# A hand-written plan of 1623 steps, in another order behind the 329th, with the loads of values issued by SyncE

## The chip, the core and the metric

The kernel runs on one core of one Trainium2 chip. The core has a matrix engine (TensorE; PE in the profile, its weight loads PEld), a vector engine (VectorE, DVE), an activation engine (ScalarE, ACT), a general engine (GpSimd, POOL) and SyncE (SP), which here issues transfers and nothing else. Each runs its own instructions in order, and they wait for one another by semaphores. Transfers between the main memory and the on-chip memory (SBUF) are carried out by 16 DMA engines; SP, ACT and POOL issue them here. TensorE writes into PSUM, a small memory whose banks the kernel names 0 to 3, beside two double ones.

The metric is the device time of one execution in microseconds, the median of several runs.

## What is computed

Four batches of eight heads, 768 positions of 64 numbers each. Every query and key is assigned to the nearest (by angle) of 16 centroids of its head, and a query attends only to the keys of its own cluster. What comes out goes, all heads side by side (512 numbers per position), through a two-layer network with SiLU between.

```python
# in _attn_ref: q_n, k_n and c_n are q, k and centroids divided by their lengths
B, H, S, D = q.shape
scale = 1.0 / np.sqrt(D)
...
q_assign = np.argmax(np.einsum('bhsd,hcd->bhsc', q_n, c_n), axis=-1)
k_assign = np.argmax(np.einsum('bhsd,hcd->bhsc', k_n, c_n), axis=-1)
mask = q_assign[:, :, :, None] == k_assign[:, :, None, :]
scores = scale * np.matmul(q, k.transpose(0, 1, 3, 2))
scores = np.where(mask, scores, -1000000000.0)
scores = scores - np.max(scores, axis=-1, keepdims=True)
attn = np.exp(scores)
attn = attn / (np.sum(attn, axis=-1, keepdims=True) + 1e-09)
return np.matmul(attn, v).astype(np.float32)
...
# in _moe_ref: x is that with the heads side by side, 3072 x 512
h = x @ w_in
g = h * (1.0 / (1.0 + np.exp(-h)))
return (g @ w_out).astype(np.float32)
```

## The kernel before

**The plan.** The kernel is scheduled by hand. After a short opening, a text of 1623 words (`plan`) is read from the first to the last, and each word is handed to `step`, which emits the instructions of one small piece of work. A word is a name, a number, and behind the point an engine letter (A for ACT, D for DVE, P for POOL) or the numbers of the PSUM banks that the step opens. Each engine gets its instructions in the order of the words, and what a step waits for follows from the tiles that it reads and overwrites. So the order of the words sets the order within each engine and each queue; between engines only the data decide, and an engine may run far ahead of another one's place in the text.

**A head, from load to output.** A job is one head of one batch (`h8` to `h31` behind the first eight, which have names of their own). Its words, in the order in which they depend on each other:

- `r` (L92) loads its queries and keys, two transfers on SP, into one of four `raw` buffers.
- `hi` (L103 on ACT, L105 on POOL, L107 on DVE) casts them to half precision; `lo` (L112, DVE) makes the rest that the cast lost.
- `ht` (L121) transposes both by a DMA transpose on SP, into `ab`. The first jobs use TensorE for that.
- `l` and `L` (L159, TensorE: 12 and 24 small matmuls) multiply with the centroids; `ls`, `mx` and `ge` (L168, L188, L197, all DVE) sum, take the maximum and mark the winner.
- From head 16 on the marks go on by `cs` (L204 and L205, POOL), `cx` (L213, a DMA transpose on SP into `cdt`) and `cv` (L217, a transfer that POOL issues) into `ab`, next to the transposed queries and keys. Before head 16 they go by `cm` (L226, TensorE), `ce` (L237 or L239) and a transfer on SP (L240).
- `qk` (L336) makes scores for 256 keys by 384 queries, two matmuls, with the marks as extra rows, so that pairs of different clusters come out hugely negative; `ex` (L341, ACT) takes the exponential into one of 13 `P` buffers. There are 192 of each. The scores go to one of two double banks.
- `vl` (L271) loads the values of a head into one of five `vn` buffers, issued by POOL where the word has the letter P, and by SP otherwise. `v` casts them (L277 on ACT, L279 on DVE or POOL) and frees that buffer.
- `pv` (L353, 36 matmuls) multiplies two heads' weights with their values; `nm` (L363 and L365, DVE) divides by the sums into one of three `xn` buffers.
- `xd` (L392) transposes that by a DMA transpose on SP into `xt`; `pt` and `pe` (L374 on TensorE, L383 or L385) do the same for some of them.

A batch has two halves of queries (`c` = 0 and 1), and four `xd` or `pe` fill `xt` of a half. The words `pv`, `nm` and `xd` count 8 for a batch: 8 to 11 are the first half of the second batch, 12 to 15 its second half, 24 and 25 the first two of the fourth.

**The network.** For the first two batches `e` (L401, four matmuls) multiplies a half's `xt` with one of 16 blocks of `w_in`, `t` (L413, ACT) takes the tanh and `g` (L416, DVE) makes the SiLU from it. The words `e48` to `e63` are the second half of the second batch. For the last two batches the first layer is done with seven products instead of eight: `ws` and `T` make sums of weights and inputs, `y` (L467, two matmuls) is one product, `u` (L479 to L483) combines them, `s` (L489, ACT) takes the SiLU. The second layer is `b` for the first rows and then `m` (L559, eight matmuls), seven products each for eleven pairs of row blocks, with `S` (L572) for the sums, `z` (L581) and `o` (L587 or L590) to bring results out and to store them (`bo`, L504, and L594, L596).

**What the letters do.** For `hi`, `v`, `ce`, `pe`, `u` and `vl` the engine letter chooses the engine. For `z` and `o` the function takes no letter:

```python
elif op == "vl":
    load_v(n, nc.gpsimd if eng == "P" else nc.sync)
elif op == "z":
    duos[n // 10].snap(n % 10)
elif op == "o":
    duos[n // 10].out(n % 10 // 2, n % 2)
```

Of the kernel before, what the change touches and what calls it, by code (L numbers as in the profile page):

```python
# [29 lines left out]
def kernel(  # L30
# [655 lines left out]
    def step(op, n, eng, banks):  # L686
# [167 lines left out]
        e53.1 t53 g53 pv16.0 nm16 qk104 ex128 ht24 g59 m22.3 qk103 ex104 ex103 S21 qk124 ht25 ex124 m21.1 z20.A hi27.D
        qk112 cs23 l24.0 e55.2 S22 ls24 mx24 S24 r28 o20 qk102 ex112 ge24 t55 g55 ex102 hi26.A lo26 m26 cv20 qk109
        ex109 z21.A qk110 pv17.0 cs22 ex110 qk108 cx22 ex108 lo27 m25 z22.A nm17 qk126 ex126 e51.3 vl23.P cv22 qk111
        vl22 t51 g51 r30 v20.P e50.2 l25.0 ex111 t50 g50 qk127 ex127 qk113 v21.D e49.3 v22.D ex113 t49 hi28.P lo28 m23
        qk116 ex116 pv18.2 g49 nm18 cs24 qk115 qk130 ls25 v23.A ex115 e52.3 t52 g52 ht26 cx23 vl30.P mx25 m31.2 ex130
        o21.A e57.0 t57 qk114 ex114 l26.3 g57 cx24 ge25 ls26 e62.1 t62 g62 cv23 qk117 ex117 e54.0 t54 g54 qk119 ex119
        e61.3 e48.1 t61 g61 vl25.P xd16 mx26 ge26 qk118 xd18 ex118 t48 g48 m27.0 o23 vl27.P vl29.P qk138 pv19.3 ex138  # L860
        ht27 cv24 qk121 ex121 cs25 m24 qk125 ex125 qk123 ex123 hi30.D S33 nm19 m37 qk122 ex122 l27.1 ws9 ws10 r29 cx25
        ht28 lo30 S43 qk120 ex120 z30.A m41.3 z40.D qk129 ex129 ls27 ht30 S31 S41 S32 xd17 pv20.1 nm20 xd19 qk142
        ex142 qk133 ex133 m36 z31.A cs26 qk132 ex132 ws0 ws1 o22 pv21.1 mx27 ge27 cs27 qk135 l28.0 ls28 S34 S42 nm21
        ex135 hi29.D qk136 m35 ex136 v27.D qk140 ex140 r31 cx27 lo29 qk134 ex134 m32.0 o30 qk137 ws2 m47 ws11 ex137
        cx26 z32.D qk143 ex143 qk139 ex139 pv22.1 qk141 o33 m33 ws4 ex141 xd21 pv23.0 ht29 mx28 nm22 S44 qk146 ex146
        ge28 cv25 qk149 ex149 nm23 xd22 l30.1 m46 z41.D v29.D cv27 qk145 ls30 xd23 ws3 hi31.D ex145 mx30 qk144 xd20
        lo31 y161.0 m45 qk155 ex144 z42.A o43 ex155 cv26 l29.1 ls29 mx29 qk147 ex147 m34 qk154 ex154 ge29 ws12 qk150
        ex150 m44 T20 qk148 ex148 o31.D ws13 ge30 T21 y167.1 u160.A u161.A y177.4 u170.D m43 ht31 cs28 T22 y171 ws5
# [59 lines left out]
```

## Time and profile before

| what | us |
|---|---|
| three runs | 297.0, 297.87, 299.0 |
| their median | 297.87 |
| the profiled execution, whole | 297.27 |
| its span, first to last instruction | 295.5 |
| PE busy, DVE, ACT, POOL | 285.6, 225.7, 241.4, 69.9 |

The profile shows one execution. The time of a run is a little longer than the span (297.27 against 295.5). "Busy" is the time in which at least one instruction of an engine ran. Matmuls overlap one another, so that the mean duration of one (326 ns for one of 384 columns) is about twice the distance at which they follow each other: in the chain of work that ended last, four such matmuls take 0.65 us. That distance is the cost of a matmul here, and the text calls it its pace. "Idle before, releaser" is the time in which an engine stood still ahead of an instruction, and what ended it. For a transfer the profile has two times: how long the queue of the issuing engine was taken by the issue, and when the data had landed, counted from the issue.

### The profile page before, as it was taken

Reading aid. Unit: us, or ns where it says so; the run is one execution under the profiler, and the core shown is the slowest. Engines: PE = TensorE matmul, PEld = TensorE weight load, DVE = VectorE, ACT = ScalarE, POOL = GpSimd, SP = SyncE. Lnnn points to the kernel's source line nnn. Section 1 sums busy time; section 2 is a strip of 40 time slices with the busy share of each in tenths; the row PEclk is TensorE's granted clock in tenths of the full one; section 3 lists DMA queues with packets and bytes.
Section 4 is the critical chain, followed back from the end, with each engine's and each line's share of the span. In section 5 each row is a group of like instructions: output and inputs, shape, how many; then the busy total and the mean of one; then the engine's idle time right before and its main releaser. Section 6 shows DMA issues by size and latency. Waiting matters only on the chain.

```text
span 295.5 us, 8542 instructions
## 1 busy us (share of the span) xinstructions
PE 285.6 (97%) x3401; PEld 209.1 (71%) x3401; DVE 225.7 (76%) x498; ACT 241.4 (82%) x422; POOL 69.9 (24%) x126
## 2 busy tenths in 40 slices
PE   8899999999999999996999999999999999999995
PEld 3767766676677887664777788766678777656884
DVE  5898949689999898887877889897756243788571
ACT  5999999965989888996998888789899999487531
POOL 2655814310200126560463202111300000000000
PEclk9999999999999999999999999999999999999999
DMA  6999999998798999795865695844100202300032
GB/s 208 289 268 248 194 205 177 231 270 184 143 311 163 215 181 183 216 234 134 182 175 173 158 144 135 102 125 133 49 10 28 78 10 75 123 3 0 14 113 89
DMA packets 75208, 44.12 MB, mean 149 GB/s; under 512 B 54289, under 2 KB 70961, under 8 KB 75169
## 3 DMA queue, kind: packets, MB, share of 16 engines
q1 hardware_dynamic: 70272, 35.75, 50.2%
q0 software_dynamic: 4608, 7.54, 13.7%
q8 instruction: 26, 0.43, 0.7%
q10 hardware_dynamic: 288, 0.30, 0.3%
q14 instruction: 14, 0.11, 0.1%
HBM read 27.30 MB, written 6.29 MB: 114 GB/s over the span
## 4 chain that ended last, share of the span: by engine, by line
PE 82%; DMA 7%; DVE 4%; ACT 3%; issue 1%; SPq 1%; DVEq 0%
PE pS L336 18%; PE xb L559 17%; PE ph L401 12%; PE pO L353 10%; PE gd L467 6%; PE psN L159 4%; DMA xt<-xn 4%; PE gx L467 3%; PE gy L467 3%; PE yb L559 3%; PE po L498 2%; ACT P L341 2%; DMA ab<-hl 2%; DVE hl L112 1%; DMA raw<-in_q_dram 1%
## 5 line engine op out<-in xcount | busy, mean ns | idle before, releaser
L341 ACT ACTIVATE P<-pS 128x768 f16<-128x768 f32 x192 | 150.2, 815 | 15.0 <-PE pS L336 13.3
L336 PE MATMUL pS<-ab 128*128 128x384 f16 x384 | 86.7, 326 | 0.6 <-ACT P L341 0.2
L401 PE MATMUL ph<-xt,win_s 128*128 128x384 f16 x256 | 49.3, 326 | 2.6 <-DMA xt<-xn 2.4
L416 DVE SCALAR_TENSOR_TENSOR gt<-tn,ph 128x384 f16<-128x384 f32 x64 | 34.2, 547 | 12.1 <-ACT tn L413 11.8
L336 PEld LDWEIGHTS <-ab 128*128 128x128 f16 x384 | 33.3, 98 | 13.8 <-issue 2.1
L353 PEld LDWEIGHTS <-P 128*128 128x128 f16 x1152 | 39.7, 97 | 4.4 <-ACT P L341 0.5
L353 PE MATMUL pO<-vt,P 128*128 128x65 f16 x1152 | 41.3, 193 | 0.0
L559 PEld LDWEIGHTS <-gt 128*128 128x128 f16 x352 | 34.3, 98 | 7.6
L401 PEld LDWEIGHTS <-win_s 128*128 128x128 f16 x256 | 24.6, 98 | 18.8 <-issue 3.3
L413 ACT ACTIVATE tn<-ph 128x384 f32<-128x384 f32 x64 | 31.1, 503 | 4.7 <-PE ph L401 4.2
L112 DVE SCALAR_TENSOR_TENSOR hl<-raw,hl 128x768 f16<-128x768 f32 (+3 forms) x35 | 32.0, 917 | 0.7 <-ACT hl L103 0.5
L559 PEld LDWEIGHTS <-s 128*128 128x128 f16 x264 | 25.6, 98 | 5.7 <-DVE s L572 0.4
L105 POOL TENSOR_SCALAR hl<-raw 128x768 f16<-128x768 f32 (+1 forms) x10 | 20.8, 2075 | 13.6 <-DMA ab<-hl 8.0
L559 PE MATMUL xb<-wout_s,gt 128*128 128x256 f16 x176 | 22.6, 272 | 0.0
L159 PEld LDWEIGHTS <-ab 128*128 128x128 f16 x544 | 18.9, 97 | 4.5 <-DMA ab<-hl 0.5
L559 PE MATMUL xb<-wc,s 128*128 128x256 f16 x160 | 20.7, 273 | 0.0
L159 PE MATMUL psN<-stk,ab 128*128 128x16 f16 (+1 forms) x544 | 19.9, 184 | 0.1
L365 DVE TENSOR_TENSOR xn<-pO,zr 128x384 f16<-128x384 f32 x32 | 17.8, 558 | 2.6 <-DMA xt<-xn 1.6
L581 ACT ACTIVATE ot<-xb 128x256 f32<-128x256 f32 x33 | 12.7, 388 | 8.0 <-PE xb L559 7.9
L572 DVE TENSOR_TENSOR s<-gt 128x1024 f16<-128x1024 f16 x22 | 15.1, 685 | 5.3 <-PE xb L559 3.1
L217 POOL DMA_DIRECT2D ab<-cdt x16 | 8.7, 545 | 42.2 <-PE pS L336 17.2
L279 POOL CAST vt<-vn 128x384 f16<-128x384 f32 x16 | 9.0, 572 | 39.9 <-DMA vn<-in_v_dram 39.4
(129 smaller groups left out, 414.3 us busy)
## 6 DMA issues: line engine op xcount, KB each, us to landing
raw<-in_k_dram SPq DMA_DIRECT2D x31, 192.0 KB, 3.9
raw<-in_q_dram SPq DMA_DIRECT2D x24, 192.0 KB, 3.9
out_dram<-ot SPq DMA_DIRECT2D x18, 256.0 KB, 2.4
vn<-in_v_dram SPq DMA_DIRECT2D x19, 192.0 KB, 4.5
vn<-in_v_dram POOLq DMA_DIRECT2D x13, 192.0 KB, 3.9
win_s<-in_moe_w_in_dram POOLq DMA_DIRECT2D x8, 256.0 KB, 6.5
wout_s<-in_moe_w_out_dram POOLq DMA_DIRECT2D x4, 512.0 KB, 7.8
out_dram<-ot SPq DMA_DIRECT2D x12, 128.0 KB, 1.7
```

Of the source, the lines that this page charges most:

```text
L105: nc.gpsimd.tensor_scalar(out=o, in0=i, scalar1=QS, scalar2=None, op0=ALU.mult)
L112: nc.vector.scalar_tensor_tensor(out=hl[:, s, 1, :], in0=raws[job.name][:, s, :], scalar=QS, in1=hl[:, s, 0, :], op0=ALU.mult, op1=ALU.sub ...
L159: nc.tensor.matmul(L[:, n % 2, :, n // 2], ab[:, i, :], stk[:, job.groups[i // 3][0], x : x + w], start=(x == 0), stop=(x + w == 2 * HC),)
L336: nc.tensor.matmul(pS[:, e, 0:HALF], abs_[kj.name][:, kn, :], rhs, start=True, stop=True)
L341: nc.scalar.activation(out=P, in_=pst.pop(u)[:, :, 0:HALF], func=AF.Exp, bias=0.0, scale=ESC)
L353: nc.tensor.matmul(o[:, (2 * t + h) * VW : (2 * t + h + 1) * VW], Ps[i + h, c, j // 2][:, j % 2, ts(t, 128)], vtb[(i + h) % 13][:, j, 0:VW ...
L365: nc.vector.tensor_tensor(out=xn, in0=ov[:, :, 0:D], in1=zr.unsqueeze(2).to_broadcast([128, 2 * NM, D]), op=ALU.mult)
L401: nc.tensor.matmul(ph[:, 0:HALF], win_s[:, r, ts(fb, 128)], xts[b, c][:, r, :], start=(r == 0), stop=(r == NR - 1))
L413: nc.scalar.activation(out=tn, in_=phs[b, c, fb][:, 0:HALF], func=AF.Tanh, bias=0.0, scale=0.5)
L416: nc.vector.scalar_tensor_tensor(out=gt[:, fb, NM * c : NM * c + NM, :].rearrange("p t n -> p (t n)"), in0=tns.pop((b, c, fb)), scalar=1.0 ...
L467: nc.tensor.matmul(o[:, 0:HALF], w[:, r, :], x[:, r, :], start=(s in (7, 1) and r == 0), stop=(r == 1), skip_group_check=True)
L559: nc.tensor.matmul(o, self.lhs(l, f), self.rhs(r, f), start=(f == 0 and opens), stop=(f == HB - 1), skip_group_check=True)
```

## The change

Up to the 329th word the plan stays as it is. From there to the end the same 1294 pieces of work stand in another order. The words are the same but for what follows the point: the banks that steps open are chosen anew, and 72 words have another engine letter. Twelve of these are `vl` (16 to 19, 21, 23 to 27, 29 and 30), which lose their P, so that SP issues them; behind the 329th word all value loads are then on SP (20, of which 8 were before). Eleven are `hi`, fourteen `v`, eleven `u`, one `ce`, one `pe`, sixteen `z` and six `o`. No function is changed.

The lines of the diff around the places that the text speaks of:

```diff
--- before.py
+++ after.py
@@ -827,69 +827,69 @@
...
-        ex39 ex40 e7.1 e12.2 t12 ht11 g15 qk41 ex41 t7 g2 r15 wc6 e9.0 hi13.P g7 qk45 ex45 v10.D pv6.3 wc0 g12 t9 qk43
-        ex43 vl26.P b0.1 nm6 g9 wc12 wc13 qk47 ex47 qk46 ex46 b1 lo13 pt6.2 qk44 ex44 pt5.3 qk42 ex42 L8.0 pe5.D mx8
-        wc14 pe6.D b2 b3 ge8 cm8 ce8.D ht13 b4.3 hi12.A bo0 L10.2 mx10 ge10 l9.0 ls9 pv7.1 wc8 b5 mx9 nm7 b6 pt7.0
-        hi14.A ge9 cm9.1 ce9.A lo12 ht12 cm10 wc9 b7 bo1 pe7.A e20.1 t20 lo14 e24.0 ce10.A ht14 g20 t24 g24 L11.3
...
-        ex50 v8.D e22.1 t22 vl9 g18 lo15 ht15 l13.0 g29 qk51 e17.3 e19.2 ls13 g22 qk52 r16 e16.0 mx13 ex51 ge13 cm13.1
...
-        qk86 o2 e37.3 cx18 ex88 ex86 o1.D hi22.P t37 ls20 qk93 g37 e41.0 ex93 qk90 ex90 cs19 cx19 nm13 r25 m12.2 o10
-        e36.3 lo22 ht22 hi23.D t41 g41 t36 qk85 ex85 g36 xd12 qk89 e44.1 e43.2 ex89 mx20 lo23 qk91 ex91 cv16 t44 qk94
-        ex94 hi24.P pv14.0 g44 ge20 e39.3 t39 r27 vl21.P e40.1 vl24.P nm14 ht23 xd13 g39 xd14 cv19 t40 qk92 l21.0 ls21
-        cs20 ex92 qk95 ex95 e34.3 t34 t43 qk96 ex96 pv15.0 qk98 ex98 g40 e38.1 v19.D mx21 ge21 g43 nm15 xd15 g34 t38
-        g38 e47.2 t47 qk97 ex97 qk101 ex101 hi25.P cs21 lo24 e45.0 l22.3 ls22 g47 mx22 qk99 cv18 ex99 e33.1 t33 g33
-        t45 qk131 ex131 l23.3 qk107 lo25 ex107 g45 e56.2 t56 ls23 e58.1 g56 t58 r26 qk100 mx23 v26.P qk105 ge23 cx20
...
-        y204 s182 s202 y203 y211 u231.D y236 vl28 s203 ws15 y227.2 cx30 y221.3 u211.A y232 s230 vl31 mx31 y216 u220.D
-        u221.D y212 s201 y222 y183 y226 s210 s220 ge31 cs31 cx31 u232 y234 y235 u212 y214 y215 cv30 v25.A m51.1 s181
-        cv29 u233 s232 u222 y224 s233 z50.A y233 y225 m61.0 u213 v30.P s212 u223 s231 s222 y213 S53 S51 S52 y223 s213
...
+        hi13.A b0.2 pt5.1 g9 pe5.D ex46 L8.3 mx8 ge8 v8.D b4.0 wc12 wc3 qk42 ex42 lo13 cm8 qk45 ex45 wc2 ce8.D b1 b2
+        L10.1 mx10 qk43 qk47 ex47 v10.D ge10 b3 cm10 b5 ht13 hi12.D lo12 ce10.D ex43 pv7.3 pt6.1 pe6.A bo0 l9.2 b6
+        ht12 nm7 pt7.1 ls9 L11.3 qk49 pe7.A mx9 ge9 cm9.2 ce9.A ex49 vl9 mx11 e27.1 qk50 ge11 hi14.D lo14 cm11 l13.2
+        ls13 mx13 ce11.A r16 ex50 hi15.A b7 bo1 t27 qk56 e20.3 t20 e22.2 ex56 qk55 ht14 ge13 cm13.0 g27 hi16.P e26.1
...
+        nm12 ge19 e47.2 vl19 qk93 ex94 g41 ex93 e42.3 qk89 t47 ex89 cs19 cx19 t42 lo23 o12 cv17 xd12 m13 o2 g47 ht23
+        o1.A hi25.D qk91 cv16 pv13.2 e38.0 ex91 g42 cx18 hi22.D lo22 o11.A ht22 t38 g38 qk86 ex86 l20.3 qk92 ex92 nm13
+        xd13 e44.1 t44 lo25 m12.0 cv19 qk95 g44 v18.A l21.2 qk90 ls20 mx20 ge20 e32.1 ex95 ex90 qk87 o10 t32 ls21 g32
+        ex87 vl17 e37.3 t37 hi24.D qk99 ex99 pv15.0 nm15 xd15 pv14.2 nm14 qk97 e34.1 l23.0 ex97 t34 v19.A g37 qk101
+        ex101 e46.2 t46 qk96 xd14 cs20 ls23 mx23 g34 lo24 g46 e36.3 e39.0 ex96 t36 g36 e43.1 t43 mx21 qk107 cv18 ex107
+        e35.2 t35 r26 g43 ge21 vl16 ge23 qk106 e33.3 l22.1 g35 ls22 t39 ex106 v17.P qk128 e63.2 t33 qk102 cx20 ex128
+        g33 e45.1 cs21 t63 qk126 g39 ws4 r27 ex102 ex126 g63 e59.3 t59 g59 e40.0 t40 g40 t45 e60.2 cv20 g45 mx22 qk98
...
+        s193 u200.D u201.D s180 s192 y237.4 u182 y202 y206 s200 u230.D y193 s191 y185 y184 y231 u202 y205 u183 s182
+        y217.4 s183 u210.A mx31 cv28 y204 y221.2 u203 y203 ge31 cs31 mx30 s202 y211 y227.3 u231.D y236 s203 vl26 v26.P
+        u220.D s201 u221.D u211.A y232 s230 vl31 u232 y212 y216 s210 y222 cx31 y226 u212 y235 s220 u222 y234 y183 s181
+        u233 s232 s233 y214 v24.D y225 y215 u223 s223 cs29 cv31 cx29 u213 ge30 y224 s213 v25.P pv24.1 y233 cs30 s212
+        s222 s231 y223 s221 y213 vl27 v27.P m51.0 s211 qk156 ex156 qk153 z50.D S53 ex153 S51 m52.3 m61.2 qk151 ex151
```

More of the change, by code (lines that the diff above doesn't have):

```diff
@@ L854 @@
[L854 to L868, printed above, removed]
@@ new lines @@
+        e29.3 t29 e17.2 t17 g18 qk57 ex57 ht15 qk59 ex59 e28.1 t28 v9.A g29 ge12 r17 wc8 g17 e24.0 cm12.3 ce12.D qk58
+        wc13 t24 g28 ex58 vl15 g24 qk51 lo16 e23.2 t23 g23 vl13 e19.3 t19 g19 ht16 L14.1 mx14 e30.0 ex51 t30 qk65 ex65
+        e31.2 g30 t31 l15.3 qk48 ex48 wc9 e16.0 ge14 cm14 ce14.A r19 ls15 qk53 t16 ex53 pv9.3 mx15 ge15 cm15.1 ce15.A
+        r20 qk63 ex63 qk77 ex77 g31 wc11 pv8.2 hi18.D hi17.D lo18 g16 qk60 ex60 e25.1 ht18 qk64 m1.0 qk68 t25 ex64
+        ex68 S3 m7 z0.A v13.P vl14 lo17 qk74 ex74 nm9 g25 S1 ht17 qk62 ex62 S2 m2.3 qk61 l16.1 ex61 qk66 ex66 m6 nm8
@@ new lines @@
+        qk70 ex70 wc14 wc15 z1.A hi19.D wc7 v15.P ls16 mx16 lo19 qk76 od2 wc10 o0 pv10.2 nm10 ex76 m5 xd8 qk67 ex67
+        qk71 r21 S13 m11.1 xd9 qk69 l17.3 hi20.D ex71 qk81 ht19 ls17 r23 mx17 ex69 m17 ex81 xd10 qk80 ex80 v14.D qk73
+        pv11.2 ex73 S4 S11 S12 z2.A o3 ge17 cs17 nm11 qk75 z10.D l18.3 ls18 lo20 ex75 qk79 hi21.D ge16 vl18 ex79 m16
+        z11.A m4 mx18 qk84 ex84 qk72 ex72 m15 lo21 qk85 ex85 r22 m3 pt11.2 pe11.A S14 qk88 ex88 l19.3 z12.D ls19 qk82
+        cx17 pv12.2 ht20 r25 e41.3 ht21 cs16 r24 ge18 qk78 ex82 ex78 t41 qk83 hi23.D ex83 o13 m14 cx16 qk94 mx19 cs18
@@ new lines @@
+        ht26 m25 z22.D ws5 qk113 cv22 ex113 g51 g49 v21.A v23.P v22.D v20.P qk112 ex112 pv17.0 qk124 ex124 nm17 ht24
+        e57.3 l25.1 t57 r28 hi28.P qk110 ex110 e48.0 ls25 qk111 mx25 ex111 ge25 m23 qk127 qk114 hi27.D ex127 pv18.1
+        o21.D ex114 g57 lo27 e54.3 t48 r31 nm18 t54 g54 qk115 ex115 l26.2 ls26 qk117 ex117 xd17 ht27 e61.1 t61 mx26
+        e56.3 qk118 l24.2 ex118 g61 ls24 qk116 ex116 mx24 cs25 cx25 cv25 g48 e52.1 t52 ge26 qk119 r30 m27.2 g52 ex119
+        qk130 ex130 pv19.0 qk122 ex122 qk125 o23 hi29.D ge24 ex125 cs24 nm19 S33 e62.1 lo28 t56 t62 m24 qk121 ex121
@@ new lines @@
+        qk123 xd19 ex123 g62 g56 m31.0 qk120 ex120 m37 qk135 ex135 ht28 pv20.1 lo29 qk138 z30.D qk132 S31 cx24 ws8 S32
+        ex138 cs26 cx26 cv26 ex132 m36 o22 qk129 ex129 S43 cv24 S41 xd18 l27.3 S34 qk143 ex143 m41.2 ls27 mx27 qk140
+        qk133 ex140 z40.D hi30.D ex133 vl24 pv21.3 qk136 z31.A S42 lo30 m46 ht29 ex136 nm21 qk137 ws6 xd21 ge27 cs27
+        cx27 ws9 m47 ex137 ws0 qk134 ex134 cv27 l28.3 m35 qk139 ls28 mx28 ht30 ge28 cs28 nm20 ws12 ws13 hi31.A m32.3
+        o30 xd20 ws1 ex139 qk141 ws10 qk142 pv22.1 nm22 z32.A o33 z41.A ws11 ex141 xd22 qk146 ex142 ex146 pv23.3 nm23
@@ new lines @@
+        lo31 qk145 qk144 ex145 m45 ex144 z42.A qk148 ws7 l29.1 ex148 qk149 ex149 o43 m33 S44 qk147 ex147 ls29 m34 xd23
+        ws14 ht31 ws15 o31.A qk150 ex150 qk154 ex154 mx29 m43 qk155 ex155 m44 T20 T21 o41.D y177.4 y167.3 u170.A o42
+        y161.1 y197.4 u160.A y171 u171.A m42.2 ws2 T22 u190.D y191 y172 cx28 y176 u161.D y162 s170 T23 s160 y166
+        u191.D o32 o40 u172 y196 y192 vl25 l31.0 y174 u162 s190 y175 y164 y165 u192 u173 s162 ws3 s173 y187.2 u180.A
+        s172 y194 y195 l30.3 u163 y163 s163 s161 ls31 ge29 ls30 y181.0 y173 y207.3 y201.1 u193 u181.A y182 y186 s171
@@ new lines @@
+        S52 S54 m56 z51.D o50 qk152 v31.D qk181 cx30 cv30 m57 S63 ex152 qk174 vl29 ex181 vl30 qk172 v29.P ex174 pv25.3
+        qk158 ex172 nm25 ex158 qk162 cv29 m67 ex162 qk165 ex165 S73 z60.A m55 z52.D v30.D S61 qk164 ex164 qk159 m62.3
+        o53 ex159 vl28 qk161 ex161 S62 m66 z61.D qk157 ex157 qk160 ex160 m53 qk171 o60 v28.D pv26.3 S64 nm26 ex171
+        qk166 ex166 qk163 m54 ex163 qk170 ex170 qk167 ex167 m65 qk178 S71 ex178 nm24 qk168 xd26 ex168 pv27.3 xd24
+        o51.A o52 qk175 ex175 qk169 m72.1 ex169 z62.A qk173 m71.0 nm27 ex173 qk189 ex189 xd27 qk177 ex177 pv28.3 nm28
@@ new lines @@
+        qk179 ex179 qk176 ex176 m63 qk183 ex183 qk185 ex185 o63 pv29.3 S72 S74 qk180 qk184 m64 nm29 z70.D ex180 ex184
+        xd25 qk182 ex182 m76 z71.D qk187 qk186 ex187 pv30.3 ex186 qk188 ex188 qk190 ex190 nm30 xd29 xd28 m75 o70 qk191
+        ex191 m77 z72.D xd30 o62 o61.D pv31.3 nm31 m73 o73 pt31.1 y241.2 m74 pe31.D T30 y257.4 u250.A T31 o72 T32
+        y247.3 y277.4 u270.D y251 u240.A u241.A y287.1 T33 y242 u251.D y271 u271.D y246 y256 s240 y252 y276 y272 o71.A
+        s250 u242 y244 s270 y245 u252 s242 u243 s243 u272 y281.0 y255 y254 u253 y243 y274 y275 u280.A u281.D y267.3
@@ new lines @@
+        s241 s252 s253 u273 u260.D s272 y261.2 y253 s251 y282 y286 s280 y273 s271 y317.4 s273 u261.D y266 y262 u282
+        y285 u310.A s260 y284 s282 y311 u311.A y297.4 u283 s283 y283 u262 y265 u290.A u263 s281 y312 y307.1 y291 s263
+        y316 y301.0 y263 u291.A y292 s310 u300.D u301.D s261 y296 s290 y264 s262 u312 y302 y306 y315 u292 s300 u302
+        y314 u313 s312 y295 y294 u293 y304 s302 S83 y305 m81.2 u303 y313 s292 m87 z80.D S81 S82 s311 S84 y303 s301
+        y293 s291 S93 m86 z81.A m82.3 m85 s293 z82.A o83 m91.1 m97 s313 s303 z90.A o80 S91 S92 m84 o82 m92.0 S103 m83
@@ L893 @@
+        S94 o81.D S101 m96 m107.3 z91.A o90 m95 m101.2 z92.D m93 z100.A S102 m106 S104 o91.D o93 m102.0 o100 z101.A
+        m105 m94 z102.D o103 m103 o92 m104 o101.D o102
     """.split()
```

39 lines of the change are left out of this document (5 added, 34 removed).

## The prediction, made before the changed kernel was run

> **What bounds the kernel now.** I read the page's first and fourth parts, then the table by stage, then the timeline and the chain in order of time around the one stage that is not full.
>
> ```profile
> span 295.5 us, 8542 instructions
> ...
> PE 285.6 (97%) x3401; PEld 209.1 (71%) x3401; DVE 225.7 (76%) x498; ACT 241.4 (82%) x422; POOL 69.9 (24%) x126
> ...
> PE 82%; DMA 7%; DVE 4%; ACT 3%; issue 1%; SPq 1%; DVEq 0%
> ```
>
> TensorE is busy 97% of the span and holds 82% of the chain that ended last. A new order removes none of its 3401 matmuls, so it can only move the time in which TensorE stands still. The common part of the two plans ends on TensorE at about 56 us; the stages behind it (columns: stretch, length, then busy time of PE, PEld, DVE, ACT and POOL, clock, DMA share, GB/s):
>
> ```profile
> 56.00:125.00 69.00, 69.00 (x898) 50.85 (x897) 61.13 (x131) 56.48 (x97) 18.33 (x29) 1.00 0.93 210
> 125.00:140.00 15.00, 12.46 (x146) 8.16 (x143) 12.09 (x26) 11.91 (x22) 4.50 (x7) 1.00 0.84 183
> 140.00:186.00 46.00, 46.00 (x615) 35.75 (x613) 38.72 (x85) 40.06 (x66) 15.87 (x29) 1.00 0.72 161
> 186.00:216.00 30.00, 29.84 (x234) 20.20 (x230) 25.80 (x55) 27.36 (x58) 5.74 (x12) 1.00 0.46 95
> 216.00:256.00 40.00, 39.58 (x522) 30.99 (x521) 17.01 (x40) 33.98 (x53) 0.00 (x0) 1.00 0.16 45
> ```
>
> PE is idle 2.54 us in 125 to 140 and 0.58 us in all the other rows together. The whole visible gain is therefore 3.1 us, and nearly all of it is one place:
>
> ```profile
> 125.16 2.32 SPq L392 DMA_TRANSPOSE xt<-xn  x1
> 128.56 1.25 PE L353 MATMUL pO<-vt,P 128*128 128x65 f16 x36
> 130.41 0.19 DVE L363 RECIPROCAL zr<-pO 128x6 f32<-128x6 f32 x1
> 131.17 4.18 SPq L392 DMA_TRANSPOSE xt<-xn  x3
> 131.63 0.56 DVE L365 TENSOR_TENSOR xn<-pO,zr 128x384 f16<-128x384 f32 x1 [1.04 <-DMA xt<-xn]
> 135.22 0.65 PE L401 MATMUL ph<-xt,win_s 128*128 128x384 f16 x3
> 138.25 0.97 PE L401 MATMUL ph<-xt,win_s 128*128 128x384 f16 x5 [2.38 <-DMA xt<-xn]
> ```
>
> Here `e56` is the first step that needs the four transposes `xd12` to `xd15`. The last product `pv15` ends at 129.8 (128.56 + 1.25). Its `nm15` takes the xn buffer that `xd12` still reads and waits 1.04 us for that landing; `xd13` to `xd15` go out in series from 131.17. The chain in order of time has the two landings, and below them the pace of each matmul:
>
> ```profile
> 119.21 0.65 PE ph L401 x4
> ...
> 121.70 0.65 PE pS L336 x4
> ...
> 125.16 6.38 DMA xt<-xn
> ...
> 134.15 4.06 DMA xt<-xn
> ```
>
> ```profile
> 52.12 1.09 PE pO L353 x36
> ...
> 59.40 0.86 PE po L498 x4
> ...
> 64.55 0.95 PE psN L159 x36
> ...
> 205.51 0.65 PE gd L467 x4
> ```
>
> `xd15` lands at 138.21, and TensorE goes on at 138.25: the stall of 2.38 us is the landing of the last transpose, nothing else.
>
> **The change part by part.** (1) *The distance from the last product to the first use of the transposes.* Steps on TensorE cost 0.65 (`e`), 0.325 (`qk`, `y`), 1.09 (`pv`), 0.86 (`b`) and 0.026 for each small matmul of `l` (12) and `L` (24). Before, six `qk`, four `e` and two `l` lie between `pv15` and `e56`: 1.95 + 2.6 + 0.63 = 5.2 us. After, the last product is `pv14`, and up to `e63`, the new first user, lie six `qk`, seven `e` and two `l`: 7.1 us. `pv15` has one `pv` more, 8.2. `xd12` now stands 18 us of TensorE work ahead of `e63`, so the buffer that `nm14` takes over from it is free. What `pv14` needs is 0.19 + 0.56 and a landing:
>
> ```profile
> DMA to landing us min/median/max: 2.3/2.6/6.4
> ```
>
> That is the line of L392 (all 22 transposes to xt). 0.75 + 2.6 = 3.4, and 0.75 + 6.4 = 7.15 at the worst, against 7.1. So the stall goes: -2.4. What is late next is no transpose, but the small idle of the other stages.
>
> (2) *The key and query transposes* (`ht` to `l`/`L`). SyncE runs ahead, so the TensorE work between the two words is the least cover. Before, `ht24`, `ht26`, `ht27` and `ht29` have 2.7, 1.8, 3.0 and 4.0 us. After, the smallest is `ht13` with 4.7 (one `pv`, two `qk`, one `e`, one `b`, `L`, `l` and 0.6 for four transposes and two small pairs), then 5.9 (`ht15`); all others have 7 or more. The landings:
>
> ```profile
> L121 SPq DMA_TRANSPOSE ab<-hl x24: 1291/1634/7511, 46.6 to 194.6; - x24
> ...
> DMA to landing us min/median/max: 3.2/4.4/11.1
> ```
>
> At the median all are covered in the new order. I take 0; a gain of up to the 0.58 idle elsewhere stays in the range. The cost if a landing is late is rival D.
>
> (3) *Twelve value loads from POOL to SP.*
>
> ```profile
> L271 SPq DMA_DIRECT2D vn<-in_v_dram x19: 328/431/1651, 7.9 to 205.8; - x19
> L271 POOL DMA_DIRECT2D vn<-in_v_dram x13: 536/557/616, 35.8 to 158.9; - x13
> ```
>
> SP issues 12 x 0.431 = 5.2 us more, POOL 12 x 0.557 = 6.7 us less. A load on SP waits for the cast that frees its buffer, with all later transposes and loads queued behind. In the new plan that cast stands 77 steps or more ahead, but for `vl30`, where it is 53, so the wait should have ended before SP comes to it. Of PE's idle 2.38 is the transposes', so loads can hold at most 0.7 of it. I take 0; at the other end, the 0.43 of one issue in front of a transpose on the path, for each of two that could stand there: +0.9.
>
> (4) *Engines.* 72 words change their engine letter. Sixteen `z` and six `o` do it without effect, since L581 and L587 to L590 do not read it. Of the rest, `hi` (the cast of keys and queries) weighs most: DVE gains four net, POOL loses three net, ACT one.
>
> ```profile
> L105 POOL TENSOR_SCALAR hl<-raw 128x768 f16<-128x768 f32 x7 | 15.6, 2233 | 8.1 <-DMA ab<-hl 8.0
> ...
> L107 DVE TENSOR_SCALAR hl<-raw 128x768 f16<-128x768 f32 x14 | 9.3, 663 | 0.0
> ```
>
> DVE: 4 x 0.66 = +2.7 spread over 56 to 190, and the other letters about balance on it. It is busy 61.1 of 69 us in the first stage, and the 7.9 idle there cover it; with that cover gone it costs the 2.7, since `l` and `pv` come behind it. POOL: 3 x 2.23 = -6.7 beside the 6.7 of the loads, on a queue that had room. I take 0.
>
> (5) *Banks.* A step that opens a bank of PSUM waits for the last read of what stood in it. Such waits are among the 0.58 us of idle that the stages show beside the stall; other numbers can save these or bring as many. I take 0, plus or minus 0.6.
>
> (6) *A new tight place.* In the new order `pv24` comes in the middle of the `y` steps. Its cast `v25` is on POOL behind `cv31`, which waits for the transpose `cx31`, which waits for `cs31` and `ge31`. From `ge31` to `pv24` lie fifteen `y`: 4.88 us. Before, nine `y`, two `qk` and 32 matmuls of four products lay there, and `v25` was on ACT. The links, from the timeline, and the cdt and cast lines of L213 and L279:
>
> ```profile
> 209.47 0.48 POOL L204 TENSOR_SCALAR od<-od 128x96 f16<-128x96 f16 x1 [5.25 <-DVE od L197]
> 209.89 0.29 POOL L205 TENSOR_SCALAR od<-od 128x96 f16<-128x96 f16 x1
> 210.10 1.11 POOL L217 DMA_DIRECT2D ab<-cdt  x2
> ```
>
> ```profile
> DMA to landing us min/median/max: 2.3/2.5/5.5
> ```
>
> ```profile
> L279 POOL CAST vt<-vn x16: 493/513/1046, 13.4 to 211.2; 128x384 f16<-128x384 f32 x16
> L279 DVE CAST vt<-vn x11: 349/352/833, 29.1 to 220.9; 128x384 f16<-128x384 f32 x11
> ```
>
> 0.71 + 2.5 + 0.55 + 0.51 = 4.3 us of 4.88: no stall at the median, 2.4 at the largest landing. By median 0, and 2.4 is the other end.
>
> The cast `v24` on DVE now stands right beside `v25` on POOL. One pair of such neighbours is in the trace:
>
> ```profile
> 126.89 2.12 POOL L105 TENSOR_SCALAR hl<-raw 128x768 f16<-128x768 f32 x1
> ...
> 128.39 0.83 DVE L279 CAST vt<-vn 128x384 f16<-128x384 f32 x1
> ```
>
> The DVE cast took 0.83 instead of 0.35 and ended 0.2 us after POOL's operation. The Trainium skill (SBUF — State Buffer, the part on the port pair that DVE and GpSimd share) says that such a pair excludes one another for a whole instruction, and the row agrees. By that rule the chain grows by 0.35 to 4.6 us: no stall at the median landing, but one from a landing of 2.75 on instead of 3.1, which would move 0.04 from the forecast to rival C. The chances below go without it.
>
> **Sum.** The profiled execution took 297.27. 297.27 - 2.4 + 0 (five times) = 294.9. That execution stands 0.6 under the median of the three runs, 297.87, so 294.9 is 1.0% under the median.
>
> **The rivals.** *A deeper gain (B).* The short idle and the waits hidden in the modelled ends go as well: 294.9 - 0.6 - 0.5 = 293.8, the 0.5 being a cast (`v31`, by the POOL row 0.51) that ACT no longer makes in the stage from 216 on, where exps pace TensorE. Against it: ACT is still busy about 33.5 of 40 there. *The wait moves (C).* `pv24` or `e63` stalls as long as `e56` did: 294.9 + 2.4 = 297.3. For it speaks the margin of 0.6 us in (6); against it the median. That is also the time if the moved loads are merely hidden and the transposes stay late. *Slower (D).* `ht13` lands late at about 70 us, where its cover is 4.7: at the 11.1 that is the largest landing, +6.4, so 301.3. It decides from a landing of 7.1, where the 2.4 are eaten. For it: DMA share 0.93 in that stage. Against it: median 4.4.
>
> **How the numbers follow.** Chances: forecast 0.58, B 0.14, C 0.16, D 0.12. About 1% is what a measurement of this kernel can tell from no change; that bound under 297.87 is 294.9, so the forecast lies on it and I split it 0.32 to 0.26. Faster 0.46 (0.32 + B), same 0.42 (0.26 + C), slower 0.12 (D). The range leaves out D's 0.12 above and 0.05 below. Its low end is B less the spread of the runs below the profiled one, 293.0. Its high end is C with the 0.9 of (3), 298.2.
>
> **What would show it.** Right: no idle of PE before L401 between 120 and 140, and xn at L365 not waiting for a landing. C: idle before L353 pO near 210, ended by a POOL cast. D: idle before L159 near 70. Wrong in (4): DVE full and PE waiting on hl or vt. The prediction is wrong if PE's idle behind 56 us does not fall by about 2.4, or if it falls and the time does not.

## The result, and the profile after

Twelve runs of the changed kernel have a median of 295.49 us, twelve of the kernel before one of 298.38. The ratio is 0.9935, with a 95% interval of 0.991 to 0.996: 0.65% faster. 294.9 was predicted, and 293.0 to 298.2 as the range. Here and below a ratio is taken from the undisturbed executions of both kernels alone (one of the changed kernel took 1649.54 us); the quotient of the two medians is 0.9903.

The page of the changed kernel, its first line, busy times and the chain by engine:

```profile
span 294.3 us, 8522 instructions
...
PE 285.3 (97%) x3401; PEld 209.0 (71%) x3401; DVE 227.9 (77%) x500; ACT 239.8 (81%) x422; POOL 59.3 (20%) x112
...
PE 83%; DMA 6%; ACT 5%; DVE 2%; issue 2%; SPq 0%; DVEq 0%; ACTq 0%
```

DVE has gained 2.2 us and POOL lost 10.6; TensorE has the same 3401 matmuls. The table by stage of the changed kernel, for the stretches shown of before (length, then busy time of PE, PEld, DVE, ACT, POOL, clock, DMA share, GB/s):

```profile
56.00:125.00 69.00, 69.00 (x885) 50.62 (x883) 64.17 (x136) 57.83 (x99) 9.87 (x17) 1.00 1.00 209
125.00:140.00 15.00, 15.00 (x172) 10.15 (x171) 12.83 (x29) 13.07 (x26) 2.52 (x6) 1.00 0.83 184
140.00:186.00 46.00, 46.00 (x611) 35.95 (x609) 39.81 (x86) 39.94 (x67) 13.74 (x26) 1.00 0.76 161
186.00:216.00 30.00, 29.91 (x263) 20.53 (x261) 25.71 (x54) 25.84 (x52) 5.52 (x12) 1.00 0.36 93
216.00:256.00 40.00, 39.65 (x493) 30.66 (x492) 18.27 (x43) 33.66 (x54) 1.57 (x3) 1.00 0.23 67
```

TensorE's idle time here has gone from 3.12 us to 0.44, and all of 125 to 140 is full. The timeline of the changed kernel around the place (start, time taken, engine, line, count; for SP the time is that of the issue), its SP, PE and DVE rows put in order:

```profile
120.61 1.21 SPq L392 DMA_TRANSPOSE xt<-xn  x1
...
126.07 2.35 PE L353 MATMUL pO<-vt,P 128*128 128x65 f16 x72
...
127.48 2.00 SPq L392 DMA_TRANSPOSE xt<-xn  x1
...
127.60 0.56 DVE L365 TENSOR_TENSOR xn<-pO,zr 128x384 f16<-128x384 f32 x1
...
128.69 0.56 DVE L365 TENSOR_TENSOR xn<-pO,zr 128x384 f16<-128x384 f32 x1
...
130.68 2.48 SPq L392 DMA_TRANSPOSE xt<-xn  x2
...
135.46 0.81 PE L401 MATMUL ph<-xt,win_s 128*128 128x384 f16 x4
```

`xd12` goes out at 120.61, `xd13` at 127.48, `xd15` and `xd14` from 130.68. No DVE row has a wait for a landing, and `e63` runs its four matmuls in one go at 135.46. The last transpose was issued at 131.95 and landed 2.3 later, 1.2 us ahead of it.

The spans differ by 1.2 us only, less than the stall. The same step of the common opening, `e9`, is 1.9 us later in the second of these two executions; first the row of before, then that of after:

```profile
55.32 0.81 PE L401 MATMUL ph<-xt,win_s 128*128 128x384 f16 x4
```

```profile
57.19 0.81 PE L401 MATMUL ph<-xt,win_s 128*128 128x384 f16 x4
```

Up to there the two kernels issue the same instructions, so this is chance (in all the profiled executions here `e9` starts between 55.3 and 57.2, whatever the order behind it): behind it the changed kernel is 1.9 + 1.2 = 3.1 us shorter.

### The profile page after: what moved, and what is told of

Same layout as the page of the kernel before. It is cut to its first block, busy times and chain, and to the rows that moved or that the text cites. A ratio compares the mean times of both kernels' runs of the same rounds, so it can differ in the third digit from the quotient of the medians.

```text
span 294.3 us, 8522 instructions
## 1 busy us (share of the span) xinstructions
PE 285.3 (97%) x3401; PEld 209.0 (71%) x3401; DVE 227.9 (77%) x500; ACT 239.8 (81%) x422; POOL 59.3 (20%) x112
## 4 chain that ended last, share of the span: by engine, by line
PE 83%; DMA 6%; ACT 5%; DVE 2%; issue 2%; SPq 0%; DVEq 0%; ACTq 0%
PE pS L336 18%; PE xb L559 17%; PE ph L401 14%; PE pO L353 11%; PE gd L467 6%; DMA vn<-in_v_dram 5%; PE psN L159 4%; PE gx L467 3%; PE yb L559 3%; ACT P L341 3%; PE gy L467 3%; PE po L498 2%; DMA raw<-in_q_dram 1%; PE wb L559 1%; ACT hl L103 1%
## 5 line engine op out<-in xcount | busy, mean ns | idle before, releaser
L336 PEld LDWEIGHTS <-ab 128*128 128x128 f16 x384 | 33.8, 98 | 15.2 <-issue 1.8
L401 PEld LDWEIGHTS <-win_s 128*128 128x128 f16 x256 | 24.6, 98 | 15.6 <-issue 0.3
L105 POOL TENSOR_SCALAR hl<-raw 128x768 f16<-128x768 f32 (+1 forms) x7 | 13.8, 1977 | 42.4 <-DMA raw<-in_k_dram 37.0
L159 PEld LDWEIGHTS <-ab 128*128 128x128 f16 x544 | 19.1, 97 | 4.3 <-issue 0.5
L467 PEld LDWEIGHTS <-win_s 128*128 128x128 f16 x128 | 12.4, 97 | 9.0 <-issue 1.4
```

The source lines that it names most:

```text
L159: nc.tensor.matmul(L[:, n % 2, :, n // 2], ab[:, i, :], stk[:, job.groups[i // 3][0], x : x + w], start=(x == 0), stop=(x + w == 2 * HC),)
L336: nc.tensor.matmul(pS[:, e, 0:HALF], abs_[kj.name][:, kn, :], rhs, start=True, stop=True)
L401: nc.tensor.matmul(ph[:, 0:HALF], win_s[:, r, ts(fb, 128)], xts[b, c][:, r, :], start=(r == 0), stop=(r == NR - 1))
L467: nc.tensor.matmul(o[:, 0:HALF], w[:, r, :], x[:, r, :], start=(s in (7, 1) and r == 0), stop=(r == 1), skip_group_check=True)
```

## The experiments

Each diff shows short stretches of the plan. "Before" beside the experiments is the kernel before, run on the same chip in turn with them; over those three sessions its medians are 299.36, 298.02 and 299.12.

**Which part of the change brings the gain.** First the new order with the twelve value loads back on GpSimd.

```diff
-        hi21.D ge16 vl18 ex79 m16
+        hi21.D ge16 vl18.P ex79 m16
...
```

> The changed order, with the twelve value loads given back to POOL; nothing else differs. Theory (the order does it, the loads are neutral): no idle of PE at L401 between 120 and 140 us, ratio to the kernel before 0.990 to 0.996, the same as the whole change within 0.3%. Rival (loads on SP do it): PE waits 2 us or more for xt at the first e of the second half, ratio 0.998 or more, and single runs above 300 us as in the kernel before.

296.28 us, ratio 0.9956 (0.9927 to 0.9985). TensorE is busy all of 125 to 140, so the order alone removes the stall. The waits of TensorE in this kernel (what waited, for what: total us, times, longest) show a new one:

```profile
PE pO L353 <- POOL vt L279: 0.6, 1, 0.6
```

That is `pv24`, the tight place of step 6, where `v25` is late. In the new order `vl26` is the word right ahead of its cast `v26.P`. On SyncE, which runs ahead there, it went out by 198.1 and `v26` did not wait; on POOL it goes out at 205.85, behind `cs31`, and the cast holds up all that POOL does next:

```profile
208.92 0.50 POOL L279 CAST vt<-vn 128x384 f16<-128x384 f32 x1 [2.46 <-DMA vn<-in_v_dram]
```

The time differs too little from the changed kernel's for a verdict; the rows say what SyncE saves in this order. One of the twelve runs took 300.81 us.

Then the new order with the longer distance undone: three products of the first layer moved back ahead of `pv15`, so that 5.2 us of TensorE work are left between the last product and `e63` instead of 7.1.

```diff
-        qk99 ex99 pv15.0 nm15 xd15 pv14.2
+        qk99 ex99 e43.2 t43 g37 e35.1 t35 g43 e36.3 t36 g35 pv15.0 nm15 xd15 pv14.2
...
```

> The changed order, but three e of the first half (e43, e35, e36) moved from behind pv14 to before pv15, so that the cover from pv14 to e63 falls from 7.1 to 5.2 us, what it was before. Theory A (distance alone decides): the wait of 2.4 us is back at e63. Theory B (distance, and the chain xd12 landing - xn buffer - four transposes in series, which the new order also eased): pv14's end to the landing of xd14 was 5.85 us in the changed kernel, so the wait is 0.6 us (0 to 1.2) and the ratio to the kernel before 0.992 to 0.998.

295.51 us, ratio 0.9927 (0.9889 to 0.9966), and no wait at `e63`. The distance alone, the prediction's reason, is not what removes the stall. The 0.6 us of theory B did not come either: the last transpose landed 4.1 us after the end of `pv14`, not 5.85. So both parts of the place were undone, the distance and the early transposes:

```diff
-        cv17 xd12 m13 o2
+        cv17 m13 o2
...
-        lo22 o11.A ht22 t38
+        lo22 o11.A ht22 xd12 t38
...
-        pv15.0 nm15 xd15
+        e43.2 t43 g37 e35.1 t35 g43 e36.3 t36 g35 pv15.0 nm15 xd13 xd15
...
```

> The new order with both parts of the place undone: three products moved back before pv15 (distance from pv14 to e63 5.2 us instead of 7.1), and xd12 issued behind ht22, xd13 behind nm15. Theory (it takes both, a short distance and late transposes, to stall): nm14 waits again for xd12 or the transposes land in a row, and a stall of 1 to 2.4 us stands before e63 again: ratio to the kernel before 0.996 to 1.002, 1 to 2.4 us above the changed kernel's 295.5. Rival (the place does not matter, the gain is from the rest of the order): no stall over 0.3 us there, 295.0 to 296.0 us.

295.56 us, ratio 0.9934 (0.9909 to 0.996): still no stall. A miss for the theory. `nm14` did wait for `xd12` and three transposes did go out in a row (timeline, rows of SP, DVE and PE):

```profile
129.21 3.79 SPq L392 DMA_TRANSPOSE xt<-xn  x3
...
129.95 0.56 DVE L365 TENSOR_TENSOR xn<-pO,zr 128x384 f16<-128x384 f32 x1 [0.70 <-DMA xt<-xn]
...
134.46 0.81 PE L401 MATMUL ph<-xt,win_s 128*128 128x384 f16 x4
```

But the row starts right behind `nm15`, no transpose of keys stands ahead of it, and the last one lands 2.3 us after its issue at 131.79, at 134.10: in time by 0.4 us.

The other way round, the old order with the longer distance was tried twice, with three products moved behind `pv15`:

```diff
-        pv14.0 g44 ge20 e39.3 t39 r27 vl21.P e40.1 vl24.P
+        pv14.0 g44 ge20 r27 vl21.P vl24.P
...
-        qk107 lo25 ex107 g45 e56.2 t56
+        qk107 lo25 ex107 g45 e39.2 t39 e40.0 t40 g39 e34.1 t34 g40 ls23 e56.3 g34 t56
...
```

> The old order, but the three steps e39, e40 and e34 of the first half moved from before pv15 to just before e56, so that seven e instead of four lie between pv15 and e56 (1.95 us more). Theory (the stall is distance): the wait at e56 falls from 2.4 to 0.4 us or less, time 1.5 to 2.5 us under the kernel before, ratio 0.992 to 0.996. Rival (the wait moves): the wait at e56 goes but PE waits as long at e39, e40, e34 or at qk and l steps near them, ratio 0.998 to 1.002.

300.53 us, ratio 1.0118 (1.0063 to 1.0173). The waits moved, as the rival had it, but the moved steps brought banks of their own into it:

```profile
PE psN L159 <- DVE xn L365: 1.2, 1, 1.2
...
PE psN L159 <- DMA ab<-hl: 1.0, 1, 1.0
PE yb L559 <- DVE gt L416: 1.0, 1, 1.0
PE ph L401 <- DVE L L168: 1.0, 1, 1.0
```

The second try chose other banks and put `e39` and `e40` ahead of `l23`:

```diff
-        qk131 ex131 l23.3 qk107 lo25 ex107 g45 e56.2
+        qk131 ex131 e39.2 t39 e40.0 t40 g39 l23.3 qk107 lo25 ex107 g45 e34.1 t34 g40 e56.2
...
```

> The old order with three products of the first layer moved behind pv15 again (e39 and e40 before l23, e34 before e56), this time on banks that are free by then; the distance from pv15 to e56 is 7.1 us as in the new order, and the transposes xd12 to xd15 stand where they stood. Theory (held buffer and transposes in a row): the stall at e56 shrinks by the 1.95 us of the moved work at most, to about 0.4 us, but the earlier steps lose their cover and 0.5 to 1.5 us come back at l21 or at other places near it: ratio 0.995 to 1.002. Rival (distance alone, as the prediction had it): no stall of over 0.3 us between 120 and 140, ratio 0.990 to 0.994.

300.56 us, ratio 1.0094 (1.0052 to 1.0136). `e40` opens the bank that `g45` reads, and on DVE `g45` now stood behind `g39`, which waits for its tanh: 2.96 us at that place. Both expectations missed. Neither try says anything clean about the distance in the old order; both show that a step moved by a dozen words brings its bank and its gate along.

**What holds the last transpose in the old order.** The first two of the four transposes were moved up, right behind the steps that make their data; the distance stayed at 5.2 us.

```diff
-        ge19 nm12 t42 g42
+        ge19 nm12 xd12 t42 g42
...
-        cx19 nm13 r25 m12.2
+        cx19 nm13 xd13 r25 m12.2
...
-        ex85 g36 xd12 qk89
+        ex85 g36 qk89
...
-        nm14 ht23 xd13 g39
+        nm14 ht23 g39
```

> The old order with two words moved: xd12 right behind nm12 and xd13 right behind nm13, so that SyncE issues these two transposes about ten steps earlier, not behind r25, ht22 and ht23. The distance from pv15 to e56 stays at 5.2 us of TensorE work. Theory (held buffer and transposes in a row): nm15 no longer waits for the landing of xd12 (1.04 us at L365 before), xd14 and xd15 alone go out late, xd15 lands within about 3.5 us of pv15's end, and the stall at e56 falls from 2.38 to 0.5 us or less: ratio 0.992 to 0.996. Rival (distance alone): the stall at e56 stays at 1.5 us or more and the ratio at 0.997 to 1.003.

295.84 us, ratio 0.9933 (0.9899 to 0.9967). Two words moved give the whole gain of the change. `e56` and the step behind it run through (x8, no wait):

```profile
132.97 2.51 SPq L392 DMA_TRANSPOSE xt<-xn  x2
...
135.90 1.71 PE L401 MATMUL ph<-xt,win_s 128*128 128x384 f16 x8
```

Then each of the two moves alone, first `xd12`:

```diff
-        ge19 nm12 t42 g42
+        ge19 nm12 xd12 t42 g42
...
-        ex85 g36 xd12 qk89
+        ex85 g36 qk89
```

> The old order with one word moved: xd12 right behind nm12. xd13 stays behind ht23, so xd13, xd14 and xd15 still go out in a row. Theory H (the held buffer: nm15 waits for the landing of xd12 and passes that on to xd15): it alone brings the gain, ratio 0.991 to 0.996, xn at L365 does not wait for a landing, stall at e56 under 1 us. Rival Q (SyncE's queue is full there, and xd15 goes out when the transposes ahead of it have been issued, not when its data are there): xd15 is issued no earlier than 134, the stall stays at about 2 us and the ratio at 0.998 to 1.004.

and `xd13`:

```diff
-        cx19 nm13 r25 m12.2
+        cx19 nm13 xd13 r25 m12.2
...
-        nm14 ht23 xd13 g39
+        nm14 ht23 g39
```

> The old order with one word moved: xd13 right behind nm13; xd12 stays behind r25 and ht22. Theory H (the held buffer): nm15 still waits about 1 us at L365 for the landing of xd12, ratio 0.998 to 1.003. Rival Q (the queue): with one transpose less ahead of xd15 in the row it is issued about 1.2 us earlier, and the ratio is 0.991 to 0.997.

`xd12` alone: 297.79 us, ratio 0.9979 (0.9913 to 1.0045). `xd13` alone: 297.19 us, 0.9972 (0.9915 to 1.0028). The times don't separate them; the timelines do. SP and PE with `xd12` early:

```profile
128.87 3.45 SPq L121 DMA_TRANSPOSE ab<-hl  x1
132.37 4.20 SPq L392 DMA_TRANSPOSE xt<-xn  x3
...
139.26 0.97 PE L401 MATMUL ph<-xt,win_s 128*128 128x384 f16 x5 [1.89 <-DMA xt<-xn]
```

and with `xd13` early:

```profile
129.90 2.06 SPq L121 DMA_TRANSPOSE ab<-hl  x1
132.05 2.84 SPq L392 DMA_TRANSPOSE xt<-xn  x2
...
135.81 0.52 PE L159 MATMUL psN<-stk,ab 128*128 128x32 f16 x12 [1.06 <-DMA ab<-hl]
...
136.50 1.46 PE L401 MATMUL ph<-xt,win_s 128*128 128x384 f16 x8
```

With `xd12` early no DVE row waits for a landing, yet three transposes still queue behind `ht23`, the last goes out at 135.37, 2.5 us after its data are there (132.90), and the stall stands. With `xd13` early two queue there, and `e56` runs through; a late landing of `ht23` costs 1.06 at `l23` instead. So the held xn buffer, my theory at that point, falls as the cause of this stall. That the last transpose goes out when what stands ahead of it on SyncE's queue has been issued, as the rival had it, is what the traces show. But the queue alone doesn't tell stall from no stall: counted from the end of `pv15`, `xd15` goes out after 4.3 us in the kernel before, 3.8 with `xd12` early, 3.5 with `xd13` early and 3.8 with both. What differs most is the landing: 4.1 and 3.9 us where there is a stall, 2.5 and 2.3 where there is none.

The kernel before, unchanged, once more:

> The kernel before, unchanged, to have a second profiled execution of it. If the stall at e56 is a matter of where SyncE issues xd15, it is again 2 to 2.6 us. If it is the chance of one landing (4.06 us in the first profile, 2.3 the median of that line), it is anything from 0.5 to 5 us, and an execution with a long one also shows a lower granted clock behind it (0.5 to 0.65 for some 3 us, as behind the stalls of 2.96 and 4.80 us in two kernels here).

301.32 us. TensorE's rows behind the stall, and the clock by stretch of this execution (the third figure from the end is the granted clock):

```profile
139.21 1.06 PE L401 MATMUL ph<-xt,win_s 128*128 128x384 f16 x5 [2.34 <-DMA xt<-xn]
140.07 1.49 PE L336 MATMUL pS<-ab 128*128 128x384 f16 x4
141.35 3.11 PE L401 MATMUL ph<-xt,win_s 128*128 128x384 f16 x12
```

```profile
138.00:141.00 3.00, 1.79 (x8) 0.94 (x8) 1.26 (x3) 0.98 (x2) 0.00 (x0) 0.83 0.60 153
141.00:144.00 3.00, 3.00 (x13) 1.52 (x12) 1.96 (x6) 2.04 (x4) 0.00 (x1) 0.60 0.48 119
```

The stall is there again with almost the same length, 2.34 us; since the last landing was long again too (4.1), this doesn't decide between the queue and the landing. Here `nm15` did not wait for `xd12`, another sign against the held buffer. What is new stands behind the stall: four `qk` matmuls take 1.49 where they take 0.81, twelve of `e` 3.11 where 2.11 is usual. By the two rows the clock takes 3 x 0.17 + 3 x 0.40 = 1.7 us more.

That leaves the landing. The last transpose landed 4.1 us after its issue in both executions of the kernel before and 3.9 with `xd12` early, but 2.5 with `xd13` early and 2.3 with both early, in the changed kernel and in six of the other eight. Three in a row is not enough to make it slow (2.3 with both parts undone).

The traces show where the time goes. A landing is counted in sixteen parts. In the kernel before, fifteen parts of the last transpose were in 2.29 us after its issue and the sixteenth after 4.06; with `xd12` early it is 2.31 and 3.85. In both, a transfer on a queue that the profile calls `instruction` was under way just then: 16 KB, begun about 1.7 us after the issue and 1.2 and 1.0 us long, with a smaller one behind it. The queues' shares while the last transpose was in flight (packets, MB, share of the 16 engines), in the kernel before and then in the changed kernel:

```profile
q1 hardware_dynamic: 975, 0.41, 45.0%
q8 instruction: 1, 0.02, 1.8%
q14 instruction: 1, 0.01, 0.7%
```

```profile
q1 hardware_dynamic: 908, 0.29, 49.8%
```

In the second execution of the kernel before two such transfers, 1.5 and 1.4 us long, were in the flight, and all sixteen parts came late, after 3.9 to 4.1 us. With `xd13` early and in the changed kernel there was none; with both early one began 0.03 us before the landing. Over all DMA transposes of the 14 traces, 51 have a sixteenth part that comes over 0.5 us behind the thirteenth, and 50 of these have such a transfer in flight; but so have 338 that land together. So these transfers are the likely cause; no run here moves one to test it.

**The loads in the old order.**

```diff
-        g24 L11.3 vl17.P v17.A e27.2
+        g24 L11.3 vl17 v17.A e27.2
...
-        r27 vl21.P e40.1 vl24.P nm14 ht23
+        r27 vl21 e40.1 vl24 nm14 ht23
...
```

> The old order, with the twelve value loads on SP; nothing else differs. Theory (loads neutral): PE still waits about 2.4 us (1 to 4) before L401 at e56, ratio 0.997 to 1.005, runs scattered as widely as those of the kernel before (8 us between lowest and highest of twelve). Rival (loads on SP do it): ratio 0.996 or less and the runs within 2 us of each other. A second rival (each load on SP delays the transposes queued behind it): wait at e56 over 4 us, ratio above 1.005.

307.25 us, ratio 1.0331 (1.0266 to 1.0395): slower by 3.3%. The second rival had the direction (above 1.005), but not the size, and not the larger of the two places. The timeline, SP, ACT, DVE, PE, and the clock behind it:

```profile
74.64 0.57 SPq L271 DMA_DIRECT2D vn<-in_v_dram  x1
...
77.57 0.52 ACT L277 ACTIVATE vt<-vn 128x384 f16<-128x384 f32 x1 [5.96 <-DMA vn<-in_v_dram]
...
78.51 0.56 DVE L416 SCALAR_TENSOR_TENSOR gt<-tn,ph 128x384 f16<-128x384 f32 x1 [5.62 <-ACT tn L413]
...
79.12 2.72 PE L401 MATMUL ph<-xt,win_s 128*128 128x384 f16 x8 [4.80 <-DVE gt L416]
```

```profile
79.00:82.00 3.00, 2.88 (x15) 1.50 (x15) 3.00 (x7) 2.61 (x6) 0.00 (x0) 0.50 0.08 21
```

In the old order `vl17` is the word right ahead of its cast `v17.A`. On GpSimd's queue it ran far ahead of its place (in the kernel before it went out by 59.7); on SyncE's it waits its turn and goes out at 74.64. ACT stands 5.96 us at the cast with the tanh of the network behind it, DVE waits for the tanh, TensorE for the gate that reads its bank. A second wait of 2.26 us, at `l23`, comes from `vl21` and `vl24` ahead of `ht23`.

The nine others alone, with `vl17`, `vl21` and `vl24` left to GpSimd (the diff against the kernel with twelve):

```diff
-        g24 L11.3 vl17 v17.A e27.2
+        g24 L11.3 vl17.P v17.A e27.2
...
-        r27 vl21 e40.1 vl24 nm14 ht23
+        r27 vl21.P e40.1 vl24.P nm14 ht23
```

> The old order with nine of the twelve value loads on SyncE; the three that stayed with GpSimd are vl17, which stands directly ahead of its cast in the old order, and vl21 and vl24, which stand ahead of ht23. With all twelve on SyncE the time was 307.25 us (ratio 1.0331). Theory (the load that has its cast close behind it, and loads ahead of a transpose that TensorE needs soon): the waits of 4.8 us at e29 and of 2.3 us at l23 are gone, and the ratio is 0.997 to 1.006. Rival (SyncE is simply too full with twelve more issues): the ratio stays at 1.015 or more, with waits for landings spread over other places.

299.57 us, ratio 1.0053 (1.0007 to 1.0098). The 4.80 and the 2.26 are gone, so three loads made 2.8 of the 3.3%. In this execution the held xn buffer did cost something, at `nm15` and on TensorE behind it:

```profile
133.39 0.56 DVE L365 TENSOR_TENSOR xn<-pO,zr 128x384 f16<-128x384 f32 x1 [1.89 <-DMA xt<-xn]
...
134.00 0.81 PE L401 MATMUL ph<-xt,win_s 128*128 128x384 f16 x4 [1.01 <-DVE xn L365]
```

At `e56`, where the last transpose landed 2.3 us after its issue, it did not stall. The Trainium skill (DMA: Bandwidth & Descriptors, "Issuing engines are not separate DMA queues") says that issuing from several engines only saves the time to initiate, usually small. The rows agree that a load's issue is small (0.57), but not that little hangs on the engine: its place in a queue did.

**The letters in the old order.** Of the 72, the 38 of `hi`, `v`, `ce`, `pe` and `u`, nothing else:

```diff
-        t12 ht11 g15 qk41 ex41 t7 g2 r15 wc6 e9.0 hi13.P g7 qk45 ex45
+        t12 ht11 g15 qk41 ex41 t7 g2 r15 wc6 e9.0 hi13.A g7 qk45 ex45
...
```

> The old order, banks and loads, with the 38 letters of hi, v, ce, pe and u of the changed kernel (the letters of z and o have no effect). Theory (step 4 of the prediction: costs nothing, gains nothing): ratio 0.997 to 1.003, with the stall at e56 still there. Rival (the casts moved from POOL to DVE hold up DVE in 56 to 125): ratio over 1.005 with PE waiting for hl, vt or psN; or (ACT, relieved of v17 and v25, paces the end less): ratio under 0.996.

305.87 us, ratio 1.0243 (1.0165 to 1.0321). The largest loss in 56 to 125 is not the DVE's of the rival, but one of ACT. Its row, and TensorE's behind it:

```profile
58.88 0.84 ACT L103 ACTIVATE hl<-raw 128x768 f16<-128x768 f32 x1 [1.66 <-DMA ab<-hl]
...
60.47 0.48 PE L336 MATMUL pS<-ab 128*128 128x384 f16 x2 [1.28 <-ACT P L341]
```

`hi13`, on ACT, waits 1.66 us for a transpose that still reads its buffer, with the exponential `ex45` behind it. The new order puts `hi13.A` ten words later. TensorE waits 1.28 and 0.60 us here, and behind that the granted clock fell to 0.50 for some 3 us. More waits, for ACT and for DVE, stand in 186 to 216, where TensorE is busy 27.9 of 30 us. The stall at `e56` is not in this execution, whose TensorE had lost over 5 us before it came there.

## Why the prediction was right, and where its reasons were not

- **What bounds the kernel, and the stall**: right. The idle before `e56` was nearly all of the visible loss, and it is gone.
- **(1) The distance**: the right result by a reason that does not hold by itself. "What `pv14` needs is 0.19 + 0.56 and a landing" was the mis-sized term: 3.4 us were set down, 5.85 were needed (128.42 to 134.27), because `xd14` left the queue 2.7 us after its data were there. The 7.1 still covered it. And at the old distance of 5.2 the stall did not return (0.9927). In the old order the same stretch took 8.4 us, or 8.05 in the second execution: by the views of before, 2.4 to the end of `nm15`, 2.0 in the queue and 4.06 for the landing, of which 1.77 is its one late part. Without that part about 0.6 of the 2.38 would have been left (an estimate, 2.38 less 1.77). The prediction saw the wait of `nm15` and the row of three, and worked with neither; for the landing it took the median of 2.6, and 6.4 at the worst. Moving `xd12` and `xd13` up, named only in passing, is enough for the gain; in its profiled execution the last transpose went out 0.5 us earlier, counted from `pv15`, and landed 1.7 us faster. With a landing as long as 4.06 the new order would have needed 7.6 us (5.85 + 1.75), more than the 7.1, so it is in part luck that its landing was a quick one.
- **(2) Key and query transposes**: right, as far as its tightest place shows. `ht13` landed 4.2 us after its issue at 67.59, 0.6 us ahead of `l13` at 72.43. Rival D did not come.
- **(3) The loads**: 0 was near enough for the new order (with the loads on POOL, one stall of 0.6), and the reason was half of one. I looked at the cast that frees a load's buffer, not at the distance from a load to its own cast, nor at what a load on SyncE holds back. In the old order three such loads are 2.8 of the 3.3%; in the new order the same happens on POOL, with `vl26`. Which queue runs ahead of its place depends on the order.
- **(4) The letters**: the same. 0 fits the new order, whose trace shows no wait of TensorE over 0.3 us behind the opening; the old letters in the new order were not run. In the old order the new ones cost 2.4%. The bound of 2.7 by DVE looked at the busiest engine; the largest single loss was one cast on ACT that waits ahead of an exponential.
- **(5) Banks**: no wait on a bank over 0.3 us is left in the changed kernel's trace, inside the plus or minus 0.6. The two tries with late products show what a wrong bank costs.
- **(6) `pv24`**: no stall, with 0.3 us to spare: `v25` ended at 210.50 and its neighbour `v24`, which `pv24` needs as well, at 210.72; `pv24` began at 211.03. With the loads on POOL it stalled 0.6, so the margin was as thin as said.
- **Sum and rivals**: the sum stood on the bound of 1%, and the measured 0.65% lies on its side of no change. A gain of 2.4 was forecast from one profiled execution, and the medians differ by 2.9; that they come so close is in part luck. The 0.5 is not one term: the opening varies by as much, and many runs of the kernel before pay more than the stall, as below. That a new order "can only move the time in which TensorE stands still" left out the clock: against the runs of the kernel before at full clock (297.1, below) the gain is 1.6. The low end of the range doesn't follow from its words, since the lowest run is only 0.27 under the profiled one (293.5, not 293.0). B's deeper gain and C's full wait did not come.

## What to carry to other kernels

Where transfers go out on one queue, follow the last one a matrix product waits for back through everything issued ahead of it, not only to its data, and forward to the last part of its landing; a transfer moved up behind its producer can be worth as much as a new order of the work. An engine letter or a queue is priced together with its place: ask what the moved piece waits for there, and what stands behind it. And undo a reason, not only a change: with the distance put back, the time stayed.
